# One more product of block 0 done by the inner scheme, with its operands' homes and part of a layer norm moved

## The chip, the cores and the metric

The kernel runs on one core of one Trainium2 chip. The metric is device time in microseconds (us) of an execution, as the median over runs. The engines are named by their hardware names: TensorE (PE, with its weight loads as PEld), VectorE (DVE), ScalarE (ACT), GpSimd (POOL) and SyncE (SP), which here only issues DMAs.

## The reference

A layer norm without affine part, then a two-layer MLP over the channels:

```python
y = _layernorm(x, axis=-1)                           # (x - mean) / sqrt(var + 1e-5)
h = _gelu(jnp.einsum("bsd,df->bsf", y, w1) + b1)     # tanh form
return jnp.einsum("bsf,fd->bsd", h, w2) + b2
```

Here x is 1 x 2048 x 1024, w1 is 1024 x 3584, w2 is 3584 x 1024, all bf16.

## The kernel before

The 2048 rows are two blocks of 1024 rows (s = 0 and 1). Each block runs the layer norm, a first matmul (w1, then gelu into h) and a second matmul (w2).

Both matmuls use a 2 x 2 fast scheme with seven products in place of eight (Strassen in Winograd's form). Rows and columns are split in quarters 11, 12, 21, 22, and the operands of products 3 to 7 are sums of quarters. For h these sums are called S1 to S4, and for w2 they are T1 to T4 (`w2_prep` makes T1 to T4 once, in block 0, and stores them to `w2_sums` in DRAM). In the second matmul the products run in the order `SEQ2 = (1, 5, 2, 6, 7, 3, 4)`.

A product of the second matmul is done in one of two ways. A *plain* product (`plain`, matmul on L978) is four tiles of 14 matmuls of 128x512. An *inner* product (`inner`, matmul on L1063) applies the seven-product scheme once more: seven parts (M71, M75, M76, M72, M77, M73, M74 for product 7) of 14 matmuls of 128x256. An inner product needs sums of its own on VectorE: four of the h operand (`iS5`, `iS6`, `iS7`, `iS3`, L854, 128x1792 each) and four of the w2 operand in `inner_sums` (`iT57`, two of them in one instruction on L1022, 128x3584; `iT6` and `iT4`, L854; with `split` the first is made as two, `iT5` and `iT7`). It then needs its results taken out of the accumulator banks, some by ScalarE copies (L962) and some by VectorE adds (L942). Parts 1, 2 and 3 need no w2 sum. `INNER` lists which products are inner: in block 0 products 1, 5, 2, 3, 4, in block 1 all seven.

Memory is tight, and most buffers have several lives. The w2 sums of inner products 1, 2 and 3 of block 0 lie in `Y0`, the slots of w1's chunks 5 and 6, and product 5's lie in chunk 4's slot and the output staging. The h sums lie in `X0`, the buffer of w1's sums. Results on their way lie in 12 snapshot slots of 128x512 f32 (`snaps`; holders `g1`, `g5`, `g12`, `g3` take four each). The w2 sums made in block 0 are stored to `w_inner_sums` in DRAM (`is7_0` would be product 7's first) and read again in block 1. For products 6 and 7, which are plain in block 0, block 1 itself loads T2 or T3 to the x tiles' buffer, makes the sums (`t_inner`, L1370) and stores them.

Block 1's layer norm runs beside block 0's work, mainly on ScalarE. For tile i, `ln_act2` issues `sum`, `nm`, `sq` (L469 to L474), then `vpe` (L482), `rstd` (L485) and `nb` (L488) on GpSimd, one column of numbers each, and then `y` on ScalarE (L491), which writes the normalised tile in place into `x_sb`. The tile is then transposed by two DMAs (`yt1_i_0` and `yt1_i_1`, L520). Tile 5 is the last of the eight. `y_sums` (`yS1` to `yS4`, L543) makes the quarter sums of the transposed tiles.

In block 1's first matmul, products P1 and P2 of a unit (L767) need only raw quarters of w1 and y, and the other products need sums of VectorE. The 14 units take their w1 in seven chunks, through three slots; `w1_use` lists who must be done with a slot before the next chunk is loaded.

The order of the work is computed, not written by hand. Every operation is added with its engine, an estimated cost, its dependencies and a due time, `ORDER` adds a few microseconds to the due time of single operations, and `Planner.place` then puts each engine's operations in one order. On the chip each engine follows its list in order and waits on semaphores.

Of the kernel before, what the change touches and what calls it, by code (L numbers as in the profile page):

```python
# [6 lines left out]
ALU = mybir.AluOpType  # L7
# [16 lines left out]
P = 128  # L24
# [8 lines left out]
INNER = ((1, 5, 2, 3, 4), SEQ2)  # L33
# [6 lines left out]
    G1_5g_0_5:5.5 G1_5g_1_5:8.8 G2_5g_0_3:-15.8 G2_5g_1_3:0.8 G3_5g_0_3:7.3 G3_5g_0_5:-4.7 G3_5g_1_1:-25.3  # L40
    G4_5g_1_1:13 G6_5g_0_5:-21 G7_5g_0_3:9.2 G7_5g_0_5:6.5 M11_1:8.3 M15_0:17 M24_0:-3.1 M27_1:5.7 M43_0:-8.5
    M47_0:7.7 M51_1:7.2 M57_0:16.8 M6_0_0:3.3 M72_1:-20.2 O12_0_1:11.2 O12_0_3:8.4 P1_0_6:10.3 P1_0_9:-1.1
    P1_1_2:-2.7 P1_1_3:-18.7 P1_1_6:0.2 P2_0_12:-1 P2_0_5:0.7 P3_0_10:-9.9 P3_0_11:5.1 P3_0_12:-7.3 P3_0_2:-10.3
    P3_1_6:9.8 P4_0_3:7.4 P4_0_9:-17.7 P4_1_0:40.5 P4_1_1:54.4 P4_1_3:2 P6_0_12:-3.6 P6_0_4:1.1 P6_1_11:4.1
    P7_0_6:-33.7 c7_0_11:2.3 c7_0_5:1.2 c7_0_8:-5.5 c7_0_9:8.4 c7_1_12:9.1 c7_1_13:1.2 g12_1_1:13.1 g12_1_3:2.2
    g21_1_8:25.8 g22_0_2:1.3 g22_0_3:1.6 gS0_5g_1_3:20 gS1_5g_0_3:-6.6 gS1_5g_0_5:11.2 gS3_5g_0_5:14.9 g_0_3_2:-14.6
    hS2_0_1:-7.5 hS3_1_0:8.3 hS4_0_1:-4.8 hS4_0_3:39 iS3_1_1_0:41 iS3_2_0_0:8.3 iS5_3_1_0:28.6 iS5_4_0_0:-14.1
    iS5_5_0_0:-10 iS6_5_0_0:-3.7 iT4_1_0_0:4.1 iT4_2_0_0:3.8 iT4_3_0_0:13.3 iT5_3_0_0:14.2 iT6_1_0_0:4.6
    iT6_2_0_0:1.3 iT6_4_0_0:6.6 iT6_5_0_0:-8.9 k5_3_1:16.7 k5_5g_0_5:35.6 o12_3_0:-17 pT1_2:-34.8 pT1_3:15 pT1_6:4.8
    pT2_1:1.7 pT2_2:7.7 pT3_3:10.8 pT3_5:-2.2 pT4_0:-7.2 pT4_3:-4.3 pT4_4:-7 pT4_5:-2.4 pT4_6:7.9 plain_0_7_2None:35  # L50
    plain_0_7_3None:8.5 pw2_0:-4.4 r11_5g_1_5:-18.2 r12_5_0:10.8 r22_1_0:14.3 r22_5g_0_3:33.7 s2_2_0:-7.2
    sd1_0_2:11.5 sn1_0_9:12.1 sn1_1_10:2.8 sn1_1_5:-0.5 sn5_0_4:-29.1 st0_5_0:-3.9 w1T13_1_0:3.4 w1T1_0_4:30.1
    w1T1_0_6:-5.1 w1T1_1_2:3.5 w1T2_1_1:26.1 w1T3_0_6:-17.7 w1T4_1_3:15 w1_0_0_1:9.9 w1_0_3_0:-7.9 w1_0_5_0:-24
    w1_0_5_1:-0.6 w1_1_0_0:0.7 w1_1_6_1:-1.9 w6_0_11:-4.1 w6_0_5:-9.5 w6_1_5:-44.2 wi5_3:20.8 x0_0_1:-11.2 x1_0:4.8
    y1_6:-8.5 yS1_1_0:6.2 yS2_0_0:8.2 yS2_1_0:-3.4 yS4_1_0:8.6 yi13_1:14.5 yi2_0:-15 yt0_6_0:-2.3
# [5 lines left out]
LAT = 0.12  # L61
PE_LAT = 0.2
# [43 lines left out]
class Planner:  # L106
# [42 lines left out]
    def place(self):  # L149
# [12 lines left out]
        while left:  # L162
# [35 lines left out]
            free[e] = r + c  # L198
# [60 lines left out]
def bass_standalone__mixer_channel_mlp__prompt_kernel(  # L259
# [24 lines left out]
    with ExitStack() as es:  # L284
# [20 lines left out]
        nhalf = sb("nhalf", [P, 1], F32)  # L305
        st_sb = sb("st_sb", [P, NT, 12], F32)
# [75 lines left out]
        c_nh = add("POOL", 0.1, lambda e: e.memset(nhalf[:, :], -0.5), (), -8, "nhalf")  # L382

# [14 lines left out]
        def warm(n, deps, prio):  # L398
# [8 lines left out]
                                                    identity=identb[0:FT, 0:FT]), ())], (c_idb, b1_ld), 11.0, "b1t",  # L407
# [52 lines left out]
        junk_last = []  # L460

        junk1 = h[22][:, NU - 2:NU, :]

        def ln_act2(s, i, prio, war=None):
# [14 lines left out]
            if junk is junk1:  # L479
                for u in (NU - 2, NU - 1):  # L480
                    h_head.setdefault((22, u), []).append(a2)
            vp = add("POOL", 0.2, lambda e: e.tensor_scalar(out=vpe_sb[:, i:i + 1], in0=st_sb[:, i, 0:1],  # L482
                                                           scalar1=1.0 / D, scalar2=LN_EPS, op0=ALU.mult, op1=ALU.add),
                     (a2,), prio + 0.003, f"vpe{s}_{i}")
            rs = add("POOL", 0.6, lambda e: e.tensor_tensor(out=rstd_sb[:, i:i + 1], in0=vpe_sb[:, i:i + 1],  # L485
                                                            in1=nhalf[:, :], op=ALU.pow), (vp, c_nh), prio + 0.004,
                     f"rstd{s}_{i}")
            nb = add("POOL", 0.3, lambda e: e.tensor_tensor(out=st_sb[:, i, 1:2], in0=mv_sb[:, i, 1:2],  # L488
                                                            in1=rstd_sb[:, i:i + 1], op=ALU.mult), (rs, a1), prio + 0.005,
                     f"nb{s}_{i}")  # L490
# [82 lines left out]

        def w1_t1(s, c, prio):
            n = s * NC + c
            T1_of[(s, c)] = add("DVE", 0.65, lambda e: e.tensor_tensor(
                out=t1_sb[:, n % 2, 0].rearrange("p k (v c) -> p k v c", v=2), in0=w1raw(n, 0, 1), in1=w1raw(n, 0, 0),
                op=ALU.subtract), [w1_ld[(s, c)][0], *t1_use.get(n - 2, {}).get(1, ())], prio, f"w1T1_{s}_{c}")

        def w1_sums(s, c, prio):  # L580
# [3 lines left out]
            war = t1_use.get(n - 2, {})  # L584

            def tt(k, x0, x1, deps):
                return add("DVE", 0.65, lambda e: e.tensor_tensor(out=tv(k), in0=x0, in1=x1, op=ALU.subtract),  # L587
                           [*deps, *war.get(k, ())], prio + 0.5 * k, f"w1T{k}_{s}_{c}")

            if n > 1 and (s, c) not in GROUPED:  # L590
                raw = w1_sb[:, n % N_W1].rearrange("p k c -> p (k c)").rearrange("p (j v e c) -> p j v e c", j=2, e=2, c=P)
                T1 = T3 = add("DVE", cost2(2 * KH * 2 * P), lambda e: e.tensor_tensor(
                    out=t1_sb[:, n % 2, 0:3:2].rearrange("p a k (v c) -> p a (k v) c", c=P), in0=raw[:, :, :, 1, :],
                    in1=raw[:, 0].rearrange("p v e c -> p e v c"), op=ALU.subtract),
                    [*ld, *war.get(1, ()), *war.get(3, ())], prio + 0.5, f"w1T13_{s}_{c}")
# [10 lines left out]
        def mm1_plain(c, prio):  # L606
# [3 lines left out]
            for b in range(2):  # L610
                hold = [Holder(banks) for _ in range(4)]
                done = {f: [] for f in range(4)}
                for i in range(b * TH, (b + 1) * TH):
                    t = i % TH
                    y = y_in[(0, i)]
                    for j, f in ([(j, f) for j in range(2) for f in range(4)] if i == 0 else
# [7 lines left out]
                        o = add("PE", len(ks) * MM128, fn, list(dict.fromkeys([*done[f][:1]] + [d for _, dd in fn for d in dd])),  # L624
# [244 lines left out]
        x_gate = {}  # L869
        PU = 2  # L870
# [58 lines left out]
        def mm2_block(s, W):  # L929
# [10 lines left out]
            last_ = {}  # L940
            done = lambda p: users[p]
# [10 lines left out]
            def bank_q(h_):  # L952
                return ps[:, h_.k, :].rearrange("p (v c) -> p v c", v=2)
# [82 lines left out]
            def inner(p, a, Yo, xb, war, O=None, bias=None, out=None, gate=(), ogate=(), kk=None, tmp=None, tail=False):  # L1036
# [21 lines left out]
                subs, ev = {}, {}  # L1058

# [68 lines left out]
                k1 = copy(kk_q, lambda: bank_q(c0), (subs[1], *gate), end(1), f"k1_{nm}", alloc=hk or tmp)  # L1128
# [55 lines left out]
            def last_block():  # L1184
# [82 lines left out]
                give(hold[7], sub7)  # L1267
                for i in range(2):
# [6 lines left out]
                        (okq[q], okq[q + 1], *O12.values()), pt[7] + 7 * SUB + 0.1 * i, f"o22_{s}_{i}", alloc=ho,  # L1275
# [7 lines left out]
            def war_of(subs, p=None):  # L1283
                return {(c, r): [subs[r]] + ([ti_st[p][r]] if c == "T" and r in ti_st.get(p, {}) else [])
                        for c in "ST" for r in subs}
# [41 lines left out]
            B[4] = load_w2(s, "H", "T4", done(6) + flat(S3, S4), pt[1] + 0.1, late=3.0)  # L1327

            M7 = plain(7, S3, B[7], hb, False, [(o,) for o in O12])
            w1_use[n - 2] = w1_use[n - 2] + [M7[1]]  # L1330
            g3 = Holder(snaps, 4)
            O3 = []
            for t in range(TH):
                ho = Holder(outs)
                at = pt[7] + (t + 1) * SLOT2
                f = dve(lambda e, t=t, ho=ho: plus(e, o_sb[:, ho.k, :].rearrange("p (j c) -> p j c", j=2), bank_t(hb[t]),
                                                   tile_of(g5, t)), (M7[t], *ok_t[t // 2]), at, f"o22_{s}_{t}", alloc=ho,
                        frees=(g5,) if t == TH - 1 else ())
                store(22, t, 1, ho, (f,), at)
                O3.append(copy(lambda t=t: tile_of(g3, t), lambda t=t: bank_t(hb[t]), (f, *O3[:1]), at + 0.7, f"O3_{s}_{t}",  # L1340
                               alloc=g3 if t == 0 else None, frees=(hb[t],)))

            sub3 = inner(3, S4, inner_sums(3, B[3], Y0, war_of(sub2, 2), True), X0, war_of(sub2), O=(g12, {11: O12[1], 12: O12[1], 21: O12[3], 22: O12[3]}), out=12)
            for m in (n - 1, n):
                w1_use[m] = w1_use[m] + done(3) + kept[3]
            for m in (n - 1, n):
                for k in range(1, 5):
# [5 lines left out]
                  halves(h_flat[21]), war4, O=(g3, {11: O3[1], 12: O3[1], 21: O3[3], 22: O3[3]}), out=21)  # L1353
# [3 lines left out]
            return {"A": done(3), "B": done(4) + kept[4], "C": done(2), "ring": ring, "p5": done(5), "p2": done(2), "outs": stores}  # L1357
# [49 lines left out]
        for s in range(NSB):  # L1407
# [29 lines left out]
            else:  # L1437
                x_end = [o for i in range(NT) for o in x_free[(s, i)]] + wfree["outs"]
                e6 = t_inner(6, 1, x_end + w1_use[NC], base1[s] + 0.2 * T_MM1)
                e7 = t_inner(7, 2, e6 + w1_use[NC + 2], base1[s] + 0.45 * T_MM1)  # L1440
                W = {"A": wfree["A"], "B": wfree["B"], "x": e7, "C": last}
            wfree = wf = mm2_block(s, W)
            if s + 1 < NSB:
                for c in range(N_W1):
                    load_w1(s + 1, c, base2[s] + 40 + c)
                for i in range(NT):
# [5 lines left out]
                    dma_T(s + 1, i, base2[s] + 20 + 6.3 * i, ((*last, *(wf["C"] if i >= TH else ())), last))  # L1452
                y_sums(s + 1, base1[s + 1] - 4, wf["C"])
# [59 lines left out]
```

## Time and profile before

| what | value |
|---|---|
| median of 5 runs | 338.95 us (338.49 to 341.44) |
| the profiled execution | 339.63 us, of which the program's span is 337.81 us |
| TensorE clock granted in the span | 0.999 |
| TensorE busy | 330.6 us |
| VectorE busy | 281.6 us |
| ScalarE busy | 173.3 us |
| GpSimd busy | 22.3 us |
| DMA | 89.47 MB, 265 GB/s on average |

Block 0's first M part starts at 96.9 us and its last one (M44) ends at 180.2 us. The first products of block 1 stand among its last parts, from 173.5 us on. Matmuls are pipelined and their recorded ends are modelled, so the distance between two starts tells more than the duration of one. A line number can be a helper's: L854 makes all sums of `sums`, L942 all adds of `dve`, L962 all copies of `copy`.

### The profile page before, as it was taken

The page shows a single profiled execution, that of the slowest core. Times are in us where ns is not written, and L with a number is a line of the kernel's source. Part 1 is how long each engine was busy: PE and PEld are TensorE (multiplying, and loading weights), DVE is VectorE, ACT ScalarE, POOL GpSimd, SP SyncE. Part 2 cuts the span into 40 slices and gives each one's busy share as a digit, 9 for nine tenths or more (in the row PEclk, how much of TensorE's full clock was granted, in tenths as well). Part 3 has the DMA queues.
Part 4 walks back from the last instruction along what each step waited for, and adds up shares of the span by engine and source line. Part 5 has one row for each costly group of instructions (what it writes and reads, how often), then busy time and mean ns, then how long its engine had stood idle before and what let it go on. Part 6 is the DMA issues. An engine that isn't in the chain of part 4 may idle for free.

```text
span 337.8 us, 6035 instructions
## 1 busy us (share of the span) xinstructions
PE 330.6 (98%) x2399; PEld 224.2 (66%) x2399; DVE 281.6 (83%) x381; ACT 173.3 (51%) x292; POOL 22.3 (7%) x47
## 2 busy tenths in 40 slices
PE   4999999999999999999999999999999999999996
PEld 4977445545468885547875545544545888888885
DVE  3886889998999989989999978886638879999984
ACT  5575878577876688612113666765675522010200
POOL 2330110000020412300000000000000000000000
PEclk9999999999999999999999999999999999999999
DMA  7895999798868999899959549839971999999104
GB/s 212 287 189 148 356 360 316 262 312 282 259 255 286 357 367 359 212 259 385 363 177 334 163 197 315 292 129 297 345 239 54 373 322 382 331 327 302 62 2 126
DMA packets 80310, 89.47 MB, mean 265 GB/s; under 512 B 15130, under 2 KB 67226, under 8 KB 79770
## 3 DMA queue, kind: packets, MB, share of 16 engines
q1 hardware_dynamic: 80138, 88.95, 81.5%
q8 instruction: 19, 0.31, 0.4%
q10 hardware_dynamic: 144, 0.13, 0.1%
q14 instruction: 9, 0.07, 0.1%
HBM read 61.81 MB, written 24.38 MB: 255 GB/s over the span
## 4 chain that ended last, share of the span: by engine, by line
PE 90%; DMA 4%; ACT 3%; POOL 1%; issue 1%; DVE 1%; SPq 0%
PE ps L767 39%; PE ps L1063 34%; PE ps L978 7%; PE ps L619 5%; PE ps L692 4%; DMA w_sb<-in_w_dram 4%; POOL st_sb L488 1%; ACT t_sb L474 1%; PE ps L504 1%; ACT t_sb L469 1%; PE ps L1068 0%; ACT sn_sb L962 0%; ACT ps L962 0%; ACT x_sb L491 0%; SPq L350 0%
## 5 line engine op out<-in xcount | busy, mean ns | idle before, releaser
L767 PE MATMUL ps<-yw_sb,t_sb 128*128 128x512 f16 x336 | 80.0, 379 | 0.1
L767 PE MATMUL ps<-yw_sb,w_sb 128*128 128x512 f16 x312 | 74.7, 379 | 0.0
L792 ACT ACTIVATE h_sb<-ps,b_sb 128x512 f16<-128x512 f32 x78 | 52.9, 686 | 37.0 <-PE ps L767 32.3
L767 PEld LDWEIGHTS ps<-yw_sb,t_sb 128*128 128x128 f16 x336 | 32.7, 98 | 36.1 <-DVE ps L807 0.8
L767 PEld LDWEIGHTS ps<-yw_sb,w_sb 128*128 128x128 bf16 x312 | 30.3, 98 | 33.2 <-ACT ps L780 0.3
L854 DVE TENSOR_TENSOR h_sb<-h_sb 128x2048 f16<-128x2048 f16 (+2 forms) x36 | 38.6, 1085 | 7.3 <-ACT h_sb L792 5.3
L962 ACT COPY sn_sb<-ps 128x512 f32<-128x512 f32 x27 | 15.5, 583 | 32.9 <-DVE o_sb L942 18.2
L1063 PE MATMUL ps<-w2a_sb,h_sb 128*128 128x256 f16 (+1 forms) x252 | 30.3, 273 | 0.0
L942 DVE TENSOR_TENSOR sn_sb<-ps,sn_sb 128x512 f32<-128x512 f32 x35 | 24.0, 688 | 5.3 <-PE ps L1063 4.5
L1063 PEld LDWEIGHTS ps<-w2a_sb,h_sb 128*128 128x128 f16 x252 | 24.7, 98 | 3.9
L942 DVE TENSOR_TENSOR o_sb<-ps,sn_sb 128x512 bf16<-128x512 f32 (+1 forms) x29 | 19.3, 670 | 6.3 <-PE ps L1063 3.7
L978 PE MATMUL ps<-w2a_sb,h_sb 128*128 128x512 f16 x112 | 24.5, 379 | 0.0
L1063 PE MATMUL ps<-w_sb,t_sb 128*128 128x256 f16 x196 | 23.4, 273 | 0.1
L962 ACT COPY ps<-sn_sb 128x512 f32<-128x512 f32 x12 | 7.1, 589 | 30.3 <-PE ps L1063 24.6
L780 ACT COPY ps<-ps 128x512 f32<-128x512 f32 x26 | 14.9, 577 | 14.6 <-PE ps L767 14.5
L587 DVE TENSOR_TENSOR t_sb<-w_sb,t_sb 128x1024 f16<-128x1024 bf16 x26 | 17.9, 688 | 3.7 <-DMA w_sb<-in_w_dram 2.5
L1063 PEld LDWEIGHTS ps<-w_sb,t_sb 128*128 128x128 f16 x196 | 19.0, 98 | 2.7 <-ACT sn_sb L962 0.4
L792 ACT ACTIVATE h_sb<-sn_sb,b_sb 128x512 f16<-128x512 f32 x26 | 18.5, 716 | 4.0 <-DVE sn_sb L821 3.0
L807 DVE TENSOR_TENSOR ps<-ps,sn_sb 128x512 f32<-128x512 f32 x26 | 17.6, 694 | 3.3 <-PE ps L767 3.1
L978 PEld LDWEIGHTS ps<-w2a_sb,h_sb 128*128 128x128 f16 x112 | 10.9, 98 | 12.8
L619 PE MATMUL ps<-yw_sb,w_sb 128*128 128x128 f16 x256 | 17.4, 231 | 1.0 <-DMA w_sb<-in_w_dram 1.0
L619 PEld LDWEIGHTS ps<-yw_sb,w_sb 128*128 128x128 bf16 x256 | 16.3, 104 | 2.3 <-DMA w_sb<-in_w_dram 1.3
(125 smaller groups left out, 483.9 us busy)
## 6 DMA issues: line engine op xcount, KB each, us to landing
w_sb<-in_w_dram SPq DMA_DIRECT2D x28, 512.0 KB, 5.9
x_sb<-in_w_dram SPq DMA_DIRECT2D x21, 256.0 KB, 5.8
w_sums<-x_sb SPq DMA_DIRECT2D x21, 256.0 KB, 3.6
w2a_sb<-w_inner_sums SPq DMA_DIRECT2D x12, 448.0 KB, 7.2
x_sb<-in_x_dram SPq DMA_DIRECT2D x15, 256.0 KB, 6.8
w_inner_sums<-w_sb SPq DMA_DIRECT2D x4, 896.0 KB, 8.5
x_sb<-w_sums SPq DMA_DIRECT2D x2, 1792.0 KB, 9.0
w_sb<-w_inner_sums SPq DMA_DIRECT2D x8, 448.0 KB, 7.2
```

The source lines that it names most:

```text
L587: return add("DVE", 0.65, lambda e: e.tensor_tensor(out=tv(k), in0=x0, in1=x1, op=ALU.subtract), [*deps, *war.get(k, ())], prio + 0.5 * k, ...
L619: fn = [(lambda e, b=b, hb=hold[f], f=f, k=k, t=t: e.matmul(ps[:, hb.k, t * P:(t + 1) * P], lhsT=lhs[:, k, f * P:(f + 1) * P], rhs=yop[f"A ...
L692: fn = [(lambda e, k=k, v=v: e.matmul(ps[:, bank[r].k, v * QN:(v + 1) * QN], lhsT=xo()[:, k, v * P:(v + 1) * P], rhs=yv()[:, k, :], start= ...
L767: fn = [(lambda e, k=k: e.matmul(ps[:, hold[p].k, :], lhsT=lhs[:, k, :], rhs=yop[yo][:, k, :], start=(first and k == 0), stop=(k == KH - 1 ...
L780: return e.copy(out=dst, in_=src) if o_.eng == "ACT" else e.tensor_copy(dst, src)
L792: r = h_ok[(s, q, u)] = add("ACT", 0.70, lambda e: e.activation(out=dst, in_=src(), func=ACT.Gelu_apprx_tanh, bias=b1_sb[:, f:f + 1], scal ...
L807: o2 = add("DVE", 0.7, lambda e: e.tensor_tensor(out=b5v(b5), in0=b5v(b0), in1=v5(), op=ALU.add), (P6, *o5), pt[7] - SLOT, f"w6_{nm}", all ...
L854: o = add("DVE", cost2(w * dst.shape[-1]), lambda e, k0=k0, k1=k1: e.tensor_tensor(out=dst[:, k0:k1, :], in0=a[0][:, k0:k1, :], in1=b[0][: ...
L942: plus = lambda e, out, x, y: e.tensor_tensor(out=out, in0=x, in1=y, op=ALU.add)
L962: return act(lambda e: e.copy(out=out(), in_=src()), deps, at - 5, name, **k)
L978: fn = [(lambda e, k=k, t=t: e.matmul(ps[:, banks_[t].k, :], lhsT=a[0][:, k, t * P:(t + 1) * P], rhs=b[0][:, k, :], start=(first and k == ...
L1063: fn = [(lambda e, k=k, j=j: e.matmul(ps[:, bank[r].k, j * HI:(j + 1) * HI], lhsT=x[0][:, k, j * P:(j + 1) * P], rhs=y[0][:, k, :], start= ...
```

## The change

- Product 7 of block 0 becomes inner. Its w2 sums take the home `Y0` after product 2's, its h sums take `X0`, and its sums are stored to DRAM for block 1 (`is7`). Block 1's `t_inner` for product 7 goes: one load of 1.8 MB, three sums and three stores.
- The four banks of product 6 are copied out by ScalarE (`U`, in place of `O3`), and quarter 22 is finished by two wide adds (128x1024) instead of four.
- Product 7's first copy `k1_7` goes to x tile 7's buffer. Product 3's w2 sums go to the buffer of x tiles 0 to 6, so both must wait until those tiles of block 1 have been transposed (`x_late`).
- The slots of w1's chunks 5 and 6 are freed after product 7 instead of after product 3.
- In block 1's layer norms, `vpe` and `nb` run on ScalarE. Tile 5's `nb` waits for `k1_7`.
- The planner counts 0.08 us (VectorE) and 0.09 us (ScalarE) less for each operation, the entries of `ORDER` are others, b1's transpose is due earlier, and some dependencies are added where a buffer's earlier reader had not been named. Among the `ORDER` entries that go is one that delayed the load of the second half of w1's chunk 0 (`w1_0_0_1`).

```diff
-INNER = ((1, 5, 2, 3, 4), SEQ2)
+INNER = ((1, 5, 2, 7, 3, 4), SEQ2)
...
-    ... w1_0_0_1:9.9 ...
+    ...
+OVL = {"DVE": 0.08, "ACT": 0.09}
...
-            free[e] = r + c
+            free[e] = r + c - OVL.get(e, 0.0)
...
-            vp = add("POOL", 0.2, lambda e: e.tensor_scalar(out=vpe_sb[:, i:i + 1], in0=st_sb[:, i, 0:1],
-                                                           scalar1=1.0 / D, scalar2=LN_EPS, op0=ALU.mult, op1=ALU.add),
+            vp = add("ACT", 0.2, lambda e: e.activation(out=vpe_sb[:, i:i + 1], in_=st_sb[:, i, 0:1], func=ACT.Identity,
+                                                        bias=epsc[:, :], scale=1.0 / D), (a2, c_eps), prio + 0.003,
...
-            nb = add("POOL", 0.3, lambda e: e.tensor_tensor(out=st_sb[:, i, 1:2], in0=mv_sb[:, i, 1:2],
-                                                            in1=rstd_sb[:, i:i + 1], op=ALU.mult), (rs, a1), prio + 0.005,
+            nb = add("ACT", 0.2, lambda e: e.mul(st_sb[:, i, 1:2], mv_sb[:, i, 1:2], rstd_sb[:, i:i + 1]), (rs, a1),
...
-            M7 = plain(7, S3, B[7], hb, False, [(o,) for o in O12])
-            w1_use[n - 2] = w1_use[n - 2] + [M7[1]]
-            g3 = Holder(snaps, 4)
-            O3 = []
+            gu = Holder(snaps, 4)
+            U = []
             for t in range(TH):
-                f = dve(lambda e, t=t, ho=ho: plus(e, o_sb[:, ho.k, :].rearrange("p (j c) -> p j c", j=2), bank_t(hb[t]),
-                                                   tile_of(g5, t)), (M7[t], *ok_t[t // 2]), at, f"o22_{s}_{t}", alloc=ho,
...
+                U.append(copy(lambda t=t: tile_of(gu, t), lambda t=t: bank_t(hb[t]), (M6[t], *U[-1:]),
+                              pt[6] + (t + 1) * SLOT2, f"U_{s}_{t}", alloc=gu if t == 0 else None))
+                O12[t].frees = (hb[t],)
+                O12[t].deps.append(U[-1])
+
+            gw, okq, sub7 = inner(7, S3, inner_sums(7, B[7], Y0, war_of(sub2, 2)), X0, war_of(sub2),
+                                  O=(gu, {11: U[1], 12: U[1], 21: U[3], 22: U[3]}), kk=x_sb[:, NT - 1, :].bitcast(F32))
+            x_late.append((first_k[7], (NT - 1,)))
+            w1_use[n - 2] = w1_use[n - 2] + [sub7[5]]
...
+                f = [add("DVE", 1.22, lambda e, i=i, ho=ho, rows=rows: plus(
+                    e, o_sb[:, ho.k:ho.k + 2, :].rearrange("p v (j c) -> p v j c", j=2), rows(gw), rows(g5)),
...
-            sub3 = inner(3, S4, inner_sums(3, B[3], Y0, war_of(sub2, 2), True), X0, war_of(sub2), ...
+            Yo3 = inner_sums(3, B[3], [two(xf), *halves(xf)[2:4]], {}, True)
+            x_late.extend((o, range(NT - 1)) for o in users[3])
+            sub3 = inner(3, S4, Yo3, X0, war_of(sub7), ...
             for m in (n - 1, n):
-                w1_use[m] = w1_use[m] + done(3) + kept[3]
+                w1_use[m] = w1_use[m] + done(7) + kept[7]
...
-                e6 = t_inner(6, 1, x_end + w1_use[NC], base1[s] + 0.2 * T_MM1)
-                e7 = t_inner(7, 2, e6 + w1_use[NC + 2], base1[s] + 0.45 * T_MM1)
-                W = {"A": wfree["A"], "B": wfree["B"], "x": e7, "C": last}
+                e6 = t_inner(6, 1, x_end + w1_use[NC], base1[s] + 0.25 * T_MM1)
+                W = {"A": wfree["A"], "B": wfree["B"], "x": e6, "C": last}
...
+                y_nb[5].deps.append(wf["k7"])
+                for o, tiles in x_late:
+                    o.deps += [d for i in tiles for d in x_free[(s + 1, i)]]
```

## The prediction

> **What bounds the kernel now.** I read the engine shares of the page first, then TensorE's own waits, then the chain of waits, and last the table of busy time by stretch for the end of block 0's second matmul.
>
> ```profile
> PE 330.6 (98%) x2399; PEld 224.2 (66%) x2399; DVE 281.6 (83%) x381; ACT 173.3 (51%) x292; POOL 22.3 (7%) x47
> ```
>
> TensorE is busy all the time. Its waits are three, all before 8.5 us:
>
> ```profile
> PE ps L504 <- DVE x_sb L429: 2.5, 1, 2.5
> PE ps L400 <- POOL ones L375: 1.0, 1, 1.0
> PE ps L619 <- DMA w_sb<-in_w_dram: 1.0, 1, 1.0
> ```
>
> The chain gives start, length and owner of each piece. Read it for two things: what one product costs, and the two places where TensorE is not its own releaser.
>
> ```profile
> 115.33 2.83 POOL st_sb L488
> ...
> 122.80 0.48 ACT sn_sb L962
> 123.32 4.76 PE ps L1063 x42
> ...
> 137.18 18.13 PE ps L978 x84
> 155.31 18.34 PE ps L1063 x168
> ...
> 189.68 6.15 DMA w_sb<-in_w_dram
> ```
>
> L978 is a plain product and L1063 an inner one: 18.13/84 = 0.2158 us for a 512-column matmul, 18.34/168 = 0.1092 us for a 256-column one. Between 20 and 335 us the timeline shows matmuls starting at just this spacing, with two exceptions: at 122.9 us two starts lie 0.39 us apart instead of 0.11 (0.28 lost), and at 197.9 us 0.46 instead of 0.22 (0.25 lost). So the time is the sum of TensorE's instructions, some 8 us of head, and 0.53 us of stalls. Only a smaller sum, or a new stall, can move it.
>
> The stretch that the change rebuilds is the last 37 us of block 0's second matmul (columns: length, then busy us of each engine, granted clock, DMA share, GB/s):
>
> ```profile
> core 0: us, PE busy (x) PEld busy (x) DVE busy (x) ACT busy (x) POOL busy (x), PEclk, DMA share, GB/s
> 143.00:155.20 12.20, 12.20 (x59) 5.50 (x57) 10.37 (x13) 2.19 (x4) 0.00 (x0) 1.00 1.01 290
> 155.20:167.00 11.80, 11.80 (x110) 10.58 (x109) 11.36 (x13) 2.56 (x5) 0.00 (x0) 1.00 0.97 362
> 167.00:180.20 13.20, 13.20 (x106) 10.22 (x105) 12.05 (x16) 1.35 (x4) 0.00 (x0) 1.00 0.69 225
> ```
>
> VectorE has 33.78 us of work in these 37.2, and until 167 us the DMA engines are full. ScalarE is nearly idle.
>
> **The change, part by part.**
>
> *TensorE.* Plain product 7 of block 0 is 4 x 14 = 56 matmuls of 512 columns: 56 x 0.2158 = 12.09 us. As an inner product it is 7 x 14 = 98 of 256: 98 x 0.1092 = 10.70 us. All of it is on the path: -1.39 us. The Trainium skill speaks against this step: "TensorE: Matmul & The Clock Gate", Part 2, section Back-to-back issue gap, says that in a real stream with weight loads a 512-column matmul costs about 131 ns and a 128-column one about 81. By an estimate on a straight line between them (98 ns at 256) product 7 would go from 7.3 to 9.6 us, a loss of 2.3. The rows above say 0.2158 and 0.1092, and the sum goes by them.
>
> *VectorE in block 0.* Durations are from the groups by shape.
>
> ```profile
> L942 DVE TENSOR_TENSOR sn_sb<-ps,sn_sb 128x512 f32<-128x512 f32 x35 | 24.0, 688 | 5.3 <-PE ps L1063 4.5 <-PE ps L978 0.3
> L854 DVE TENSOR_TENSOR t_sb<-h_sb 128x1792 f16<-128x1792 f16 x14 | 15.2, 1087 | 1.3 <-PE ps L767 1.1
> L942 DVE TENSOR_TENSOR o_sb<-sn_sb 128x1024 bf16<-128x1024 f32 x2 | 2.4, 1224 | 0.1
> L1022 DVE TENSOR_TENSOR w_sb<-w2a_sb 128x3584 f16<-128x3584 bf16 x1 | 2.0, 2018 | 0.0
> ```
>
> Added for product 7: four h sums (4 x 1.087 = 4.35), three w2 sums (2.02 + 2 x 1.087 = 4.19), six evacuations (6 x 0.688 = 4.13), two wide adds for quarter 22 (2.45). Removed: four plain adds o22 (2.75). Product 3's double w2 sum is split in two before and after. Net +12.37. In the timeline an instruction starts some 0.09 us before its predecessor on VectorE ends, so 16 more instructions cost about 1.4 us less: +11.0. The stretch shrinks by 1.39 to 35.8 us and is asked for 33.78 + 11.0 = 44.8: 9.0 too many. What can take them: VectorE's idle time just before (110 to 143 us, rows of the same table: 33.0 - 9.38 - 9.18 - 12.44 = 2.0), and in 75 to 96.86 us (21.86 - 8.54 - 10.93 = 2.4, into which w2's preparation can move); and TensorE work that needs no VectorE sum. The last is block 1's products P1 and P2, 0.863 us each: before, four of them already stand among product 4's last parts (3.45 us). Four more (3.45) and the next unit's pair (1.73) can follow only if chunks 1 and 2 of w1 are there. 9.0 - 2.0 - 2.4 - 3.45 - 1.73 = -0.6. It just fits; the new order must find nearly all of it.
>
> *w1 chunks earlier.* Before, w1_1_1 and w1_1_2 wait for product 3, whose w2 sums live in their slots: issued at 175.2 to 176.7, landed at 180.5 to 184.8. Product 3's sums now lie in the x tiles, so the loads wait for product 7 and its stores: near 157 instead of 175. This is the step that makes the four further fillers possible. It costs nothing itself.
>
> *The new wait on the transposes.* Product 3's w2 sums must wait until x tiles 0 to 6 of block 1 are transposed, and tile 5 is last. Its nb waits for product 7's first copy. Product 7 starts where M6 ended in the timeline, 143.2; its first part takes 14 x 0.109 = 1.53; the copy 0.59: 145.4. Then nb 0.2 (row L472, 201 ns) and y 1.24: 146.9, where y1_5 ended at 143.43 before. Before, the two transposes landed 7.6 and 6.1 us after their issue, behind 1.8 MB of w2; with 5 to 7.6 us they land at 152.5 to 156 when issued at 146.9 to 148.7. Then iT5 1.09. M35 wants it at 143.2 + 10.7 + 1.53 = 155.4, or 157.0 if M32, which needs no w2 sum, goes first. Between 1.8 us early and 1.7 late; I take it as just met, since M32 can go first. Product 7's first copy itself now waits for tile 7's transpose (landed at 144.72 before, wanted at 144.9): met. Behind that copy on ScalarE stand product 7's seed and tile 5's nb.
>
> *SyncE and DMA.* Three stores (0.9 + 0.45 + 0.45 MB) move from block 1 to block 0, each queued on SyncE behind a VectorE sum, with stores and loads behind it; at 290 to 360 GB/s they are 5 to 6 us of full DMA engines between 143 and 167. The cover is the load of T4 (landed at 157.9, wanted at 162.1) and of w1_1_0 (162.0, wanted at 173.5). If it goes, product 4's sums are late next. Block 1 loses a 1.8 MB load and three sums (2.02 + 2 x 1.09 = 4.2 us of VectorE); TensorE waits for neither there, so 0.
>
> *Snapshots.* Product 3's first copy still needs a slot that g5 frees, now behind the last evacuation and a wide add: 153.9 + 0.69 + 1.22 + 0.59 + four hand-overs of 0.1 = 156.8. M36 wants it at 153.9 + 3 x 1.53 = 158.5. Nothing.
>
> *Layer norm.* vpe and nb go from GpSimd (means 374 and 898 ns, nb up to 2.83) to ScalarE at 0.2 each. ScalarE's nb then waits for GpSimd's rstd (0.57) with product copies queued behind it, about 0.8 us a tile. Against it stands the first stall: nb at 115.33 took 2.83, the next layer norm ran late, and k1_2 behind it held M26. Without the 2.63 us the copy is ready. -0.28, with 0 and -0.28 as ends.
>
> *The second stall.* At 197.9 VectorE had been held 1.8 us by w1_1_3, which waited for chunk 0's last use at 189.2. With chunks 1 and 2 there earlier and 4.2 us of VectorE less, the order around it is new; ends 0 and -0.25, I take -0.25, since the sums of chunks 1 and 2 need no longer wait for their loads.
>
> *Head.* w1's second half goes before x tile 3, which lands about 1.5 us later (11.26 for 9.78). Its y was ready at 13.95, its transpose ran at 15.24: cover 1.3, so 0.2 may show. b1's transpose had TensorE wait 0.2 at 10.1. Between -0.3 and +0.3, taken as 0. New ORDER entries and the planner's overlap of 0.08 and 0.09 us add no instruction.
>
> **The sum.** The profiled execution took 339.63 (span 337.81 and 1.82 around it): 339.63 - 1.39 - 0.28 - 0.25 = 337.71. The median of the runs is 0.68 below the profiled one: 337.0.
>
> **The rivals.** *VectorE saturates (slower).* If the order finds only the 2.0 us of idle time and the four further P1 and P2, 9.0 - 2.0 - 3.45 = 3.5 us of stall fall on products 3 and 4 and the first products of block 1; if not even the fillers, 7.0. From 338.95 - 1.39: 341.0 to 344.5, say 342. For it: VectorE must run above 97% for 75 us, where it ran at 91% (33.78 of 37.2) to 94% (31.0 of 33.0). Against: the two further outlets. It decides as soon as 0.6 us more than I count is lost.
>
> *The gain is eaten (no change).* Tile 5's transposes land at the late end, or product 7's stores delay T4: 0.5 to 2 us of waits at product 3 or 4, and the stalls stay. 337.6 + 0.9 = 338.5. For it: the DMA share of 1.01 in that stretch. Against: M31 and M32 as cover.
>
> That the change doesn't do what it says is no rival: the 56 matmuls go in any case.
>
> **How the numbers follow.** Less than 0.5% (1.7 us) is about what a measurement of this kernel can tell from no change. The forecast, 337.0 with its own range of 336.2 to 337.3, has 0.46; the eaten gain 0.24; saturation 0.30. Faster by over 0.5% is below 337.26: 0.46; same 0.24; slower 0.30. The range for all: below 336.2 (both stalls and 0.3 of head and more) I leave 0.05, above 342.0 0.13. So 336.2 to 342.0.
>
> **What would show it.** L978 with 56 matmuls (12.2 us), L1063 with 98 more; no GpSimd st_sb group, and L962 with no long wait before 123 us; w1_1_1 issued near 157. VectorE's busy share from 110 to 185 us near full with TensorE gapless is the forecast; TensorE waits on VectorE h_sb, t_sb or yw_sb sums are saturation; a VectorE x_sb sum waiting for the transposes with TensorE behind it is the eaten gain. A head that differs by over 0.3 us would make me wrong for a reason not counted.

## The result and the profile after

The kernel after takes 339.64 us (median of 44 runs, 337.58 to 342.62) against 338.59 us for the kernel before in the same comparison (79 runs). The ratio is 1.0035, with a 95% interval of 1.0024 to 1.0046: slower by about 1.2 us, where 337.0 us was forecast. The profiled execution took 341.44 us (span 339.7), 1.8 us above the median, so the stalls in it are larger than those of a typical execution. Where a size matters below, the ratios of many runs decide, and the profiles say where the time lies.

The page's engine shares, and from the groups by shape the plain products (columns: busy us, mean ns of one, idle time before):

```profile
PE 330.7 (97%) x2441; PEld 227.3 (67%) x2441; DVE 287.0 (84%) x389; ACT 177.2 (52%) x310; POOL 16.2 (5%) x32
```

```profile
L998 PE MATMUL ps<-w2a_sb,h_sb 128*128 128x512 f16 x56 | 12.4, 379 | 0.0
```

56 matmuls of 512 columns are left of 112, and TensorE has 42 more in all: product 7 is inner. TensorE's waits were only in the head before. Now there are others (columns: total us, times, longest; those of the head are left out):

```profile
PE ps L784 <- DMA w_sb<-in_w_dram: 1.2, 2, 0.8
PE ps L1084 <- DMA w2a_sb<-in_w_dram: 0.7, 1, 0.7
PE ps L1084 <- DVE x_sb L871: 0.4, 1, 0.4
PE ps L784 <- DVE ps L824: 0.2, 1, 0.2
```

The first line is w1's chunks, the second product 3's quarter B22, the third product 3's sums in the x tiles' home, the last an evacuation at 68 us. The chain of waits says what these waits rest on:

```profile
124.47 12.90 DMA w_inner_sums<-w_sb
...
155.26 5.76 DMA yw_sb<-x_sb
...
161.34 1.10 DVE x_sb L871
...
162.58 17.20 PE ps L1084 x154
...
234.98 7.48 DMA w_sb<-in_w_dram
...
263.74 71.83 PE ps L1084 x658
```

Before, the chain ran along TensorE from 123.3 to 189 us with no other owner. Now, from 113 to 162 us, it runs through stores, sums and transposes. The row at 155.26 is the second half of tile 5's transpose, which lands at 161.0; behind it stands VectorE's first w2 sum of product 3 (161.34), and behind that TensorE (162.58). The row at 234.98 is the second half of w1's chunk 6 in block 1. The last row gives the price of an inner matmul again: 71.83/658 = 0.1092 us.

SyncE's own list shows how these transfers came to be late. It issues one DMA behind the other (columns: start, us that the issuing took, what, count):

```profile
143.00 0.58 SPq L360 DMA_DIRECT2D w_inner_sums<-w_sb  x1
143.62 3.50 SPq L532 DMA_TRANSPOSE yw_sb<-x_sb  x2
147.17 1.19 SPq L360 DMA_DIRECT2D w2a_sb<-in_w_dram  x2
148.40 0.56 SPq L360 DMA_DIRECT2D w_inner_sums<-w_sb  x1
149.14 1.55 SPq L360 DMA_DIRECT2D w_sb<-in_w_dram  x2
150.73 6.51 SPq L532 DMA_TRANSPOSE yw_sb<-x_sb  x2
```

In order these are product 7's store `is7_0`, another tile's two transposes, B22, the store `is7_2`, w1_1_0 (chunk 0 of block 1's w1) and tile 5's two transposes. B22 was issued at 147.2, where the kernel before issued it at 143.5.

The same stretch by windows:

```profile
143.00:155.20 12.20, 12.20 (x113) 10.68 (x111) 12.13 (x17) 4.89 (x8) 0.00 (x0) 1.00 0.89 282
155.20:167.00 11.80, 9.84 (x73) 6.67 (x72) 9.19 (x11) 1.64 (x3) 0.00 (x0) 1.00 1.12 359
167.00:180.20 13.20, 13.20 (x119) 11.01 (x117) 13.16 (x16) 1.10 (x2) 0.00 (x0) 1.00 1.03 359
```

VectorE is full in the first and the last window, but in the middle one, where TensorE stands still for 2 us, it is idle for 2.6 of 11.8 us itself. Only the DMA engines are full there (1.12). So neither engine is the bound in that window: both wait for transfers.

Counting how much later each matmul starts than its width allows (0.0558, 0.1092 and 0.2158 us from start to start for 128, 256 and 512 columns) gives TensorE's lost time by place, in us. The kernels e5 and e10 are explained below.

| where | before | after | e5 | e10 |
|---|---|---|---|---|
| head, 0 to 20 us | 7.83 | 7.55 | 6.57 | 6.86 |
| 60 to 80 us | 0 | 0.42 | 0.25 | 0 |
| 80 to 150 us (first old stall) | 0.29 | 0 | 0 | 0 |
| 150 to 170 us | 0 | 2.47 | 0 | 0 |
| 170 to 200 us (second old stall) | 0.26 | 0.52 | 0.42 | 0.27 |
| 200 us to the end | 0 | 0.64 | 0.93 | 0 |
| sum | 8.38 | 11.60 | 8.15 | 7.13 |

The span without its losses is 337.81 - 8.38 = 329.43 before and 339.70 - 11.60 = 328.10 after: the work itself shrank by 1.33 us, and the losses grew by 3.22.

### The profile page after: what moved, and what is told of

Read it like the earlier page. It is cut to its first block, busy times and chain, and to the rows that moved or that the text cites. A ratio compares the mean times of both kernels' runs of the same rounds, so it can differ in the third digit from the quotient of the medians.

```text
span 339.7 us, 6127 instructions
## 1 busy us (share of the span) xinstructions
PE 330.7 (97%) x2441; PEld 227.3 (67%) x2441; DVE 287.0 (84%) x389; ACT 177.2 (52%) x310; POOL 16.2 (5%) x32
## 4 chain that ended last, share of the span: by engine, by line
PE 75%; DMA 13%; DVE 6%; SPq 2%; issue 2%; ACT 0%; POOL 0%; DVEq 0%
PE ps L784 33%; PE ps L1084 31%; PE ps L636 5%; PE ps L709 4%; DMA w_sb<-in_w_dram 4%; DMA w_inner_sums<-w_sb 4%; DMA w_inner_sums<-o_sb 3%; SPq L360 2%; DMA yw_sb<-x_sb 2%; DVE sn_sb L962 2%; DVE h_sb L871 1%; DVE t_sb L871 1%; PE ps L516 1%; DMA x_sb<-in_x_dram 1%; DVE w_sb L871 1%
## 5 line engine op out<-in xcount | busy, mean ns | idle before, releaser
L784 PE MATMUL ps<-yw_sb,w_sb 128*128 128x512 f16 x312 | 75.7, 379 | 1.4 <-DMA w_sb<-in_w_dram 1.2
L1084 PE MATMUL ps<-w2a_sb,h_sb 128*128 128x256 f16 (+1 forms) x280 | 33.5, 273 | 0.7 <-DMA w2a_sb<-in_w_dram 0.7
L1084 PEld LDWEIGHTS ps<-w2a_sb,h_sb 128*128 128x128 f16 x280 | 27.1, 98 | 5.5 <-issue 1.0
L962 DVE TENSOR_TENSOR sn_sb<-ps,sn_sb 128x512 f32<-128x512 f32 x40 | 27.0, 685 | 3.3 <-PE ps L1084 3.2
L962 DVE TENSOR_TENSOR o_sb<-ps,sn_sb 128x512 bf16<-128x512 f32 (+1 forms) x25 | 16.4, 664 | 6.0 <-ACT ps L1160 2.9
L871 DVE TENSOR_TENSOR t_sb<-h_sb 128x1792 f16<-128x1792 f16 x16 | 17.4, 1085 | 2.2 <-PE ps L784 1.3
L838 DVE TENSOR_TENSOR sn_sb<-ps,sn_sb 128x512 f32<-128x512 f32 x20 | 13.5, 685 | 2.6 <-PE ps L784 2.5
```

The source lines that it names most:

```text
L784: fn = [(lambda e, k=k: e.matmul(ps[:, hold[p].k, :], lhsT=lhs[:, k, :], rhs=yop[yo][:, k, :], start=(first and k == 0), stop=(k == KH - 1 ...
L838: c22 = add("DVE", 0.69, lambda e: e.tensor_tensor(out=v5(), in0=b5v(b0), in1=v5(), op=ALU.add), (P7, o2), pt[4] - SLOT, f"c7_{nm}")
L871: o = add("DVE", cost2(w * dst.shape[-1]), lambda e, k0=k0, k1=k1: e.tensor_tensor(out=dst[:, k0:k1, :], in0=a[0][:, k0:k1, :], in1=b[0][: ...
L962: plus = lambda e, out, x, y: e.tensor_tensor(out=out, in0=x, in1=y, op=ALU.add)
L1084: fn = [(lambda e, k=k, j=j: e.matmul(ps[:, bank[r].k, j * HI:(j + 1) * HI], lhsT=x[0][:, k, j * P:(j + 1) * P], rhs=y[0][:, k, :], start= ...
```

## The experiments

The edits act on the engines' finished lists, or (e2, e3) on the size of an operation with its planned cost left as it was, so nothing else is reordered: `move(engine, names, before)` takes operations out of an engine's list and puts them ahead of another. The theories in the expectations: Q, loads that TensorE needs land late because product 7's stores lie ahead of them in SyncE's queue; V, VectorE has too much work; N, tile 5's late `nb` delays its transposes. Times are medians with the ratio to the kernel before on the same chip and its interval.

**e1 and e2: the order of SyncE's queue, and the size of the stores.**

```diff
 # e1
+move("SP", ["w2_0_B22_0", "w2_0_B22_1"], "is7_0")
+move("SP", ["yt1_5_0", "yt1_5_1"], "is7_2")
+move("SP", ["is7_0", "is7_2"], "w2_0_T4_0")
 # e2 (order as in the kernel after)
-    st = dma(dst, src, ...
+    cut = KI * HI if p != 7 else HI // 2
+    st = dma(dst[:, :, 0:cut], src[:, :, 0:cut], ...
...
-    o = dma(d, ti[p - 1, j], ...
+    o = dma(d, ti[min(p, 6) - 1, j], ...
```

> The changed kernel with SyncE's list alone rearranged between 143 and 157 us: the two loads of B22 go ahead of is7_0, tile 5's two transposes ahead of is7_2 and of the load of w1_1_0, and is7_0 and is7_2 behind that load. Same work on every other engine in the same order. Theory Q (the DMA queue: 1.4 MB of product 7's stores and w1_1_0 stand ahead of B22 and of tile 5's transposes, so M32, P1_1_0 and M35 wait 0.9, 1.0 and 0.5 us): B22 lands by 150 instead of 155.9, w1_1_0 by 156 instead of 160.0, the transposes by 153 instead of 161.0, all three waits go, 2.4 us less than the changed kernel, about 337.2. Theory V (VectorE is saturated through products 7 and 3): M35 stays where VectorE's list lets iT5_3 start, the waits only move, at most 0.5 us less. Theory N (tile 5's nb behind product 7's first copy makes the transposes late): the loads' waits of 1.9 us go, but the transposes still end the wait before M35: about 1.9 us less at most.

> The changed kernel with product 7's three stores of w2 sums in block 0 cut to 1/14 of their columns, 1.8 MB less to DRAM between 143 and 166 us; block 1's product 7 reads product 6's sums in their place, so its part of the output is left out. The order of every engine is the same. Theory Q: 1.4 MB less ahead of w1_1_0 and the transposes are about 4 us of DMA time, 0.9 MB ahead of B22 about 2.5: all three waits (2.45 us) go, about 337.2. Theory V: no change, 339.6. Theory N: the transposes still wait for y1_5 (147.6), no change to M35's wait, at most 1.9 us less.

e1: 339.64 us, ratio 1.0034 (1.0006 to 1.0062), no gain, where theory Q had 337.2. e2: 338.0 us, ratio 0.9982 (0.9964 to 0.9999), 0.5% below the kernel after. In e1 the waits of 155 to 158 us shrank to 0.33 us, and a new one of 1.90 us came at 164.6. TensorE's waits of e1 name it, and e1's chain gives its length:

```profile
PE ps L1084 <- DMA h_sb<-w_sums: 1.7, 1, 1.7
```

```profile
154.12 12.41 DMA h_sb<-w_sums
166.53 0.05 issue
166.58 5.52 PE ps L1084 x49
```

The transfer is T4, product 4's operand. It took 12.41 us behind the 1.35 MB of `is7_0` and `is7_2`. So the order alone only hands the wait to the next load. In e2 the three stores are still issued, at the same places, but move 1/14 of the bytes: TensorE lost nothing from 80 to 170 us. So theory V, which had 339.6 for e2, falls as the cause of this stall. What costs is the stores' bytes, not SyncE's time to issue them (0.58 us for `is7_0` and 0.56 for `is7_2` in both profiles). The bytes also slow the issuing of what stands behind them: tile 5's two transposes took SyncE 4.4 us in e2, 6.5 in the kernel after, and 7.3 in e3 below, which has all the bytes and the same order.

**e3: less work for VectorE.**

```diff
-    out=dst[:, k0:k1, :], in0=a[0][:, k0:k1, :], in1=b[0][:, k0:k1, :], op=op),
+    out=dst[:, k0:k1, :cut], in0=a[0][:, k0:k1, :cut], in1=b[0][:, k0:k1, :cut], op=op),   # cut = 64 for hS4_0
```

> The changed kernel with the four sums hS4 of block 0 (h operand of product 3) made on 64 of 512 columns, the rest of S4 left out: about 3 us less work for VectorE between 135 and 150 us, in the same order. Theory V: product 7's evacuations and product 3's sums come up to 3 us earlier and the waits at M32, P1_1_0 and M35 (2.45 us) go: about 337.2. Theory Q: all three waits end with a DMA's landing (B22, w1_1_0, tile 5's transposes), which this does not touch: 339.6, within 0.3.

339.25 us, ratio 1.0016 (0.9996 to 1.0037). The losses of 150 to 170 us were 1.09 us in its profile, in place of 2.47, and they still end with w1_1_0 (0.52) and with product 3's sum behind the transposes (0.56), as theory Q has it. The gain over the kernel after (0.2%) lies inside the intervals. The smaller loss can't be put down to VectorE either: SyncE issued `is7_0` at 139.95 in this profile and at 139.38 in e2's, where VectorE's work is whole, against 143.00 in that of the kernel after, each time right behind another DMA.

**e4: tile 5's `nb` not behind `k1_7`.**

```diff
+ops_["nb1_5"].deps.remove(ops_["k1_7_0"])
+move("ACT", ["nb1_5", "y1_5"], "U_0_1")
+move("SP", ["yt1_5_0", "yt1_5_1"], "is7_0")
```

> The changed kernel with tile 5's nb no longer waiting for product 7's first copy: nb and y of tile 5 go ahead of the copy U of tile 1 on ScalarE (y ends near 141.3 instead of 147.6), and its two transposes ahead of is7_0 on SyncE. Theory N: tile 5's transposes land by 147 and the time falls by what the wait cost, up to 2.4 us, to 337.2. Theory Q: the transposes' volume only moves ahead in the full queue, B22 and w1_1_0 land as late as before or 1 us later, M32 and P1_1_0 still wait 1.9 us or more, and only M35's 0.5 goes: 339 to 340, within 0.6 of the changed kernel. Theory V: no change.

341.71 us, ratio 1.0091 (1.0061 to 1.0121), slower than the kernel after and than the 339 to 340 of theory Q. The transposes landed at 143.7 instead of 161.0, and yet TensorE lost 3.61 us from 150 to 170: B22's first half was issued at 146.66 and landed at 152.89, and the part that needs it (M31) was due at 150.8. Theory N falls. Here it is B22 that comes late: `is7_0` and four transposes stand ahead of it in SyncE's list, and in e1, without them, it was issued at 142.7.

**e5: the same bytes, behind T4.**

```diff
 # e1, and
-move("SP", ["is7_0", "is7_2"], "w2_0_T4_0")
+move("SP", ["is7_0", "is7_2"], "is7_3")
```

> The kernel after, with SyncE's order of e1 and in addition product 7's stores is7_0 and is7_2 moved behind the load of T4, ahead of is7_3 (the same 1.8 MB, only later). Theory Q (product 4's sums wait because T4 lands behind 1.35 MB of stores: in e1 it landed at 166.53, and TensorE stood still for 1.90 us at 164.57): T4 lands some 4 us earlier, at 162 to 163, the stall at 164.6 goes and no new one comes; 1.5 to 2 us less than e1, so 337.8 to 338.2 us. Theory V (VectorE's amount of work decides, the stall only moves from wait to wait): the stall shows again, on VectorE's sums, between 157 and 180; 339.3 to 339.8 as in e1. Theory W (the chunks 1 and 2 of w1, which wait for the stores to free their slot, come late instead): a stall of 1 to 2 us at 178 to 183; 339 to 340.

337.88 us, ratio 0.9984 (0.9967 to 1.0001), as theory Q had it, and 0.5% or 1.7 us below the kernel after. T4, issued at 151.8, landed at 160.5. The windows:

```profile
143.00:155.20 12.20, 12.20 (x115) 10.91 (x113) 12.16 (x17) 3.87 (x7) 0.00 (x0) 1.00 1.16 269
155.20:167.00 11.80, 11.80 (x95) 8.93 (x93) 11.66 (x13) 2.75 (x5) 0.00 (x0) 1.00 1.04 415
167.00:180.20 13.20, 13.20 (x109) 10.24 (x108) 13.16 (x17) 1.44 (x3) 0.00 (x0) 1.00 1.04 376
```

TensorE is busy throughout, and VectorE 36.98 of 37.2 us. The DMA engines are about as full as before the edit. No byte and no instruction went, only the queue's order changed, and the stall is gone. The Trainium skill's "DMA: Bandwidth & Descriptors", section Queues, rings and completion order, says that on each DMA engine the descriptors of a queue are consumed in ring order; the 12.4 and 8.7 us of T4 with and without the stores ahead of it agree with that.

**e6: more at once.**

```diff
 # e5, and
+move("SP", ["w1_1_0_0", "w1_1_0_1"], "w2_0_B22_0")
+move("SP", ["w1_1_6_0"], "wi1_1")
+move("DVE", ["w6_0_8", "w6_0_9"], "hS1_0_1")
```

> e5, and besides: w1_1_0's two halves issued before B22 on SyncE (their slot is free since product 5, the DMA engines have a gap at 139 to 143 us), the second half of block 1's chunk 6 of w1 issued right behind its first half, and VectorE's evacuations w6_0_8 and w6_0_9 ahead of the h sum hS1_0_1. By theory Q the waits for w1_1_0 (0.35 us at 157.8), for chunk 6 (0.66 at 240.8 in e1) and for w6_0_8 (0.58 at 68.1 in e1) go: 1 to 1.5 us less than e5 where e5 shows these waits, 336.6 to 337.4 us. By theory V nothing changes at the boundary and only the two outer waits go: 338.2 to 338.7. If w1_1_0's 0.9 MB delays B22 past 154 us, a stall of up to 2 us comes at 153 to 156 and the time is that of e5 or above.

342.64 us, ratio 1.0115 (1.0090 to 1.0139): much worse. The queue's own waits from 135 to 150 us, and the chain, say why:

```profile
SPq L360 <- PE ps L1084: 4.7, 1, 4.7
```

```profile
145.51 0.38 SPq L360
...
146.49 8.10 DMA w2a_sb<-in_w_dram
...
154.64 1.38 PE ps L1084 x11
```

I had taken w1_1_0's slot to be free since product 5. It is freed by M75 of product 7 as well (`w1_use[n - 2] + [sub7[5]]` in the change), so the moved load stood at the head of SyncE's list until 145.5 with B22 behind it. B22 was issued at 146.5 instead of 141.9, and TensorE stood still for 3.20 us at 151.3. The move on VectorE was no help either: it shifted a wait of 0.66 us to 71.8. The third move did its work: no loss after 200 us.

**e9 and e10: the two other new stalls.**

```diff
 # e9: e5, and
+move("SP", ["w1_1_6_0"], "wi1_1")
 # e10: e9, and
+move("DVE", ["hS1_0_1"], "w6_0_11")
```

> e5, and the second half of block 1's chunk 6 of w1 (w1_1_6_0) issued on SyncE right behind its first half, ahead of the six loads of product 1's blocks. Theory Q: in e5 this half landed at 239.01 behind 1.8 MB of those loads while TensorE wanted it at 238.2 (0.83 us lost); here it lands by 233 and the stall goes, the loads behind it have 8 us and more to spare: 0.6 to 0.8 us less than e5, 337.0 to 337.4 us. Theory V (the waits are a matter of VectorE, and this one only showed a DMA): the time stays at 337.9 and the loss of 0.8 us shows somewhere between 238 and 260 us.

> e9, and the h sum hS1_0_1 (1.22 us on VectorE) moved from in front of the evacuation w6_0_8 at 66 us to in front of w6_0_11 at 81 us, where VectorE stood idle for 0.87 us in e5; its first reader comes at 103 us. The stall at 67.7 us (0.22 us in e5, 0.39 to 0.58 in other profiles of this order) goes. By theory V, which holds good for this stretch of block 0 too, 0.35 us of VectorE's work then lies in front of w6_0_11: a stall of 0 to 0.35 us at 81 us. So 0 to 0.4 us less than e9: 336.7 to 337.3 us.

e9: 338.18 us, ratio 0.9972 (0.9953 to 0.9990), above the 337.0 to 337.4 expected and by its ratio not clear of e5. e10: 337.16 us, ratio 0.9952 (0.9933 to 0.9971). In e9 the half of chunk 6 landed at 232.7 instead of 239.0 and nothing is lost after 200 us, but its profile shows 0.71 us at 69.1, where a sum of VectorE stands ahead of an evacuation; in e10 that is gone too, and no stall came at 81 us. e10 is faster than the kernel before and the kernel after, with the change in it whole. Its engine shares and all of TensorE's waits:

```profile
PE 329.0 (98%) x2441; PEld 228.1 (68%) x2441; DVE 287.0 (86%) x389; ACT 177.3 (53%) x310; POOL 15.5 (5%) x32
```

```profile
PE ps L516 <- DVE x_sb L440: 2.4, 1, 2.4
PE ps L411 <- POOL ones L385: 1.0, 1, 1.0
PE ps L636 <- DVE yw_sb L523: 0.2, 1, 0.2
```

**e11: how much VectorE has to spare.**

```diff
 # e5, and
+for k in range(4):     # copies of an operation's record, with
+    o.fn = lambda e, k=k: e.bn_stats(out=scr[:, k, :], in_=w2x[:, k * HT:(k + 1) * HT])
+    order["DVE"].insert(order["DVE"].index(ops_["iS5_3_0_0" if k < 2 else "iS6_3_0_0"]), o)
```

> e5 with four more instructions on VectorE, whose results nobody reads: statistics over 512 columns each, two ahead of product 3's h sum iS5_3 and two ahead of iS6_3 (148 to 155 us). One such instruction took 683 ns in the profile, so some 0.6 us each with the overlap: 2.4 us. The forecast counted 0.6 us to spare on VectorE up to 180 us. Theory V as forecast (0.6 to spare): 1.8 us of stalls between 150 and 180 us on VectorE's sums or evacuations, 339.4 to 340.0 us. If VectorE has 2.4 us or more to spare: no stall, 337.9. If nothing is to spare: 2.4 us, 340.3.

340.51 us, ratio 1.0063 (1.0042 to 1.0083): 0.8%, or 2.7 us, more than e5, for 2.4 us of work. Its waits are the ones that a full VectorE makes:

```profile
PE ps L1084 <- DVE x_sb L871: 1.2, 1, 1.2
PE ps L1084 <- DVE sn_sb L962: 0.6, 1, 0.6
```

In the profile, the fastest execution of the run, the losses of 150 to 170 us are 2.11 us, 0.3 less than the work put in; the 2.7 us between the medians have an interval of some 0.9 us either way. So VectorE has at most a few tenths of a microsecond to spare, and TensorE pays for nearly all that is added.

**e7: only the layer norm's part of the change.**

```diff
 # the kernel before, with epsc set to LN_EPS on GpSimd; for i in range(8): vpe1_i right behind sq1_i and nb1_i right ahead of y1_i on ScalarE
+v.fn = lambda e, i=i: e.activation(out=vpe_sb[:, i:i + 1], in_=st_sb[:, i, 0:1], func=ACT.Identity,
+                                   bias=epsc[:, :], scale=1.0 / D)
+b.fn = lambda e, i=i: e.mul(st_sb[:, i, 1:2], mv_sb[:, i, 1:2], rstd_sb[:, i:i + 1])
```

> The kernel before, with only vpe and nb of block 1's layer norm on ScalarE (vpe right behind the sum of squares, nb right ahead of y); all other orders as before. The forecast's term: the stall of 0.28 us at 122.9 us goes, nothing comes: 0.3 us less, below what the times can tell. If ScalarE's waits for GpSimd's rstd hold product copies behind them, new stalls of 0.1 to 0.5 us appear between 75 and 150 us and the sum is zero or worse.

338.41 us, ratio 0.9992 (0.9977 to 1.0006), no difference that the times can show. In the profile the stall of 0.28 us at 122.9 is gone and nothing is lost from 20 to 195 us. The second old stall is still there (0.69 us in two pieces).

**e8: the stores alone, in the old order.**

```diff
 # the kernel before: copies of T3 from SBUF to a DRAM scratch, 0.9 MB ahead of w2_0_B22_0,
 # 0.45 MB ahead of yt1_5_0, 0.45 MB behind w2_0_T4_0
+o.fn = lambda e, n=n, m=m: e.dma_start(xs[n:n + m].rearrange("j p c -> p j c"), w2b[:, n:n + m, :])
+order["SP"].insert(order["SP"].index(ops_[before]), o)
+ops_[users_].deps.append(o)
```

> The kernel before, with three added stores of w2's T3 from SBUF to a DRAM scratch that nobody reads, 0.9 + 0.45 + 0.45 MB, issued ahead of B22, behind B22 and behind T4 on SyncE, which is where the kernel after has product 7's stores. Theory Q in its simple form (1.8 MB more between 143 and 163 us is enough): B22, the transposes and T4 land 3 to 5 us later, and TensorE waits 1 to 2.5 us between 155 and 170 us; 339.7 to 341.2 us. The prediction's term (in before's order T4 has 4 us to spare and w1_1_0 11.5, so the stores are covered): 0 to 0.5 us; 338.6 to 339.1 us. If it is the latter, what failed in the kernel after is not the volume alone but the volume with the earlier due times of its loads (w1_1_0 wanted at 156 us there and at 173.5 here).

339.25 us, ratio 1.0015 (0.9999 to 1.0032): some 0.5 us (0 to 1.1 by the interval), at the upper end of what the prediction's term gives. TensorE lost 0.51 us at 158.2. T4 landed at 160.8 instead of 157.9 and nobody waited for it; w1_1_0 landed at 164.7, 9 us before it was wanted. What showed was B22's second half (152.65 instead of 151.94): by the chain, product 3's sums on VectorE follow it, behind them an add of quarter 22 and ScalarE's copy for which M36 waits. The old order carries 1.8 MB more almost for nothing.

## Why the prediction was wrong, point by point

- **TensorE, -1.39: right.** -1.33 by the lost-time count. The 98 ns for a 256-column matmul, which the prediction estimated from the Trainium skill's figures for a real stream with weight loads ("TensorE: Matmul & The Clock Gate", Part 2, Back-to-back issue gap), do not show; 0.1092 us does.
- **SyncE and DMA, taken as covered: the step that failed.** The term gave the loads the due times of the old order ("the load of T4 (landed at 157.9, wanted at 162.1) and of w1_1_0 (162.0, wanted at 173.5)"), and with these it holds: e8 put the same bytes into the old order, and it cost some 0.5 us. But the VectorE term of the same prediction needs more P1 and P2 as fillers, and in the new order the first four stand between M32 and M35, from 156.3 in e1, instead of among product 4's last parts. With that w1_1_0 is wanted 17 us earlier and B22 3.4 (M31 at 151.7 in e1, 155.15 before), while 0.9 MB of stores lies ahead of B22 and 1.35 MB ahead of w1_1_0 and tile 5's transposes. The two terms were each worked out against another order. B22's second half landed at 155.9, where e1 starts M32, its reader, at 154.8; it took 8.1 us from its issue, little more than the 7.8 before, but was issued 3.7 us later. w1_1_0 landed at 158.5 and 160.0, even 2 us sooner than before, which would have been in time for the old order and was not for the new one. The transposes landed at 160.4 and 161.0. The new `ORDER` has the entries `is7_0:-2.3` and `w2_0_B22_1:18.3`, which favour the store over B22; what they do alone has not been tried. e2 (fewer bytes) and e5 (same bytes, later) each take this away, by 0.5% of the time: 1.7 us of the miss.
- **The new wait on the transposes, "just met": wrong by the same cause.** The late end was 156.0, and they landed at 161.0. `y` ended nearly as forecast (147.6 for 146.9), but the forecast took the transposes to be issued right behind it, at 146.9 and 148.7. SyncE had `is7_2` and w1_1_0 ahead of them and took 4.5 us to issue the first half, so it came to them at 150.7 and 155.3, and they took 9.7 and 5.8 us from there. The fillers give M35 some time (159.0 in e5, 157.0 in the forecast), but not that much. e4 shows that moving these two alone ahead doesn't help.
- **VectorE, "just fits" with 0.6 us to spare: it fits, but the 0.6 was miscounted.** By the prediction's own list 15 instructions come and four go, which makes 11 more, not 16 (the pages have 389 after and 381 before, with three fewer in block 1). So the overlap saves 1.0 us instead of 1.4, and 0.2 us are left. The runs agree with that: e5 runs 36.98 of 37.2 us on VectorE with no TensorE loss from 80 to 170 us, its first w2 sum of product 3 ends at 158.70, with M35 starting at 158.96, and e11's 2.4 us cost 2.1 in the profile and 2.7 by the medians. The rival *VectorE saturates* was not what happened: in the kernel after VectorE itself waited in the window of the stall. The earlier w1 chunks, issued near 157 in the forecast, came at 166.5, since they wait for the store `is7_3`, which landed at 166.4; they were still in time.
- **The rival that came true** is *The gain is eaten*, in its mechanism (tile 5's transposes at the late end, product 7's stores ahead of the loads). Its price, 338.5, was too low by 1.1 us: it gave the waits 0.9 us, where the ratios give 1.7, and it had no term for the stalls of the new order elsewhere.
- **First old stall, -0.28: right** (gone in the kernel after and in e7 alone). `vpe` and `nb` took 0.29 us each, not 0.2, and TensorE waited for no copy of ScalarE behind them. The snapshots, taken as nothing, cost nothing either in e5 and e10.
- **Second old stall, -0.25: not got.** Some 0.1 us pieces stand in its place, 0.27 us in e10.
- **Other orders "add no instruction": the second miss.** The new `ORDER` entry `w1_1_6_0:15.3` puts the second half of chunk 6 behind the loads of block 1's product 1, and VectorE's new order puts an h sum of 1.22 us ahead of an evacuation for which TensorE waits. In the profiles they cost 0.2 to 0.8 and 0 to 0.7 us; taking both away (e5 to e10) is 0.3% of the time, 1.1 us, with an interval of 0.1 to 0.6%; which of the two gives how much the times don't tell.
- **Head, 0: right.** 7.55 us after and 7.83 before, and over all the profiles 6.4 to 7.8 in either kernel.

By the ratios: the forecast change is 337.0/338.95, -0.6%. e10 is at -0.48%, e5 at -0.16%, the kernel after at +0.35%. So two things make up 0.83 of the 0.92% of the miss: 0.51 is the loads behind the stores, 0.32 the two stalls that the new order brought elsewhere, each known to some 0.2%. With both mended the change gives what the sum promised, within the interval.

What stays open: the kernel after varies more from run to run than the kernel before (337.6 to 342.6, against 337.6 to 341.4 and a single run of 585.7), and its profile, at 341.44, was among the slower ones. In its profile is2_0 landed at 137.4, in e2's at 132.7, with the same queue ahead of it, so its DMA backlog was longer before product 7 began. 1.3 us of that is TensorE's own lag by then (7.99 us lost up to 80 us for 6.67); where the rest comes from has not been tried. So the 2.47 us of this profile are more than the usual loss (1.7 by the ratios). The backlog alone makes no stall: in e5 and e10, with the two stores behind T4, is2_0 landed at 136.2 and 135.7, and TensorE lost nothing from 150 to 170 us there.

## What to carry to other kernels

Work out a load's slack against the due times of the new order, not of the old: where one step of a change moves a consumer earlier (a filler, a part that goes first) and another puts bytes ahead of its load, the two terms must be summed on the same transfer. In a queue that is full for tens of microseconds, what counts is which bytes stand ahead of the next wanted load; stores that nobody reads soon belong behind all loads that are wanted soon, and moving a transfer can hand the wait to the next one (e1, e4). Before a DMA is moved ahead, look up everything that its slot waits for: one that waits at the head of an in-order queue holds all behind it (e6, 4.7 us).

## What the runs showed of the hardware

- One queue's transfer pays for the bytes ahead of it: T4 took 12.4 us from issue to landing behind 1.35 MB of stores (e1) and 8.7 us without them (e5), and over the whole span of every profile here SyncE's transfers landed in the order of their issue.
- The issuing itself takes SyncE's time, and how much varies: in the kernel after a plain DMA took from 0.32 us and a transpose from 1.2, but tile 5's first transpose, at 150.7, took 4.5 us, and one at 127.3 took 7.5. These two landed 9.7 and 12.2 us after their issue began.
- With the DMA engines' share at 1.0 to 1.2, the profiles show from 232 to 415 GB/s over stretches of about 12 us; the lowest rates fall where four transposing DMAs run (143 to 155 us: 232 GB/s at a share of 1.10 in e1, 269 at 1.16 in e5).
- ScalarE took 0.29 us for one column of 128 numbers with a scale or bias read from memory (`vpe` and `nb`), where `nm`, with its constant factor, took 0.20 (both in the kernel after).
